# Holding the filter loads back until half of x has landed, with more filler matmuls in the first inverse stage

## The chip, the cores and the metric

The kernel runs on one core of a Trainium2 chip. The metric is device time in microseconds (us) of one execution. Beside the time, each execution has a span (first to last instruction, about 1.8 us less than the time) and the mean granted TensorE clock, 1.000 being full speed.

## The reference

x is [8, 3008, 256]. Along its sequence axis it goes through a real FFT, a product with a complex filter, and the inverse FFT. The result, 24064 tokens of 256, goes through a gated feed-forward layer.

```python
X = np.fft.rfft(x, axis=1)
Y = X * (filt_r + 1j * filt_i)[None]
y = np.fft.irfft(Y, n=3008, axis=1).reshape(24064, 256)
out = (np.maximum(y @ w_gate, 0) * (y @ w_val)) @ w_out      # d_ff = 1536
```

## The kernel before

The FFT is done in matmul stages. For the first of the eight batches they run one after the other, before the feed-forward stage has anything to do: **A** (psA: x times a DFT table, evicted to asb, stored to DRAM as Abuf), the reload of Abuf as **at** in another layout, **B** (psX: a small DFT of at; tt and uu: products with the filters Ftr and Fti; psD: the inverse, with the tables I2t and I2u; evicted to dsb, stored as Dbuf), and C (psY). I2t is a rearranged F2 and I2u is I2t times a permutation, both built on chip while the loads run. Fillers ("junk", psJ) are matmuls whose results nobody reads; they are there to keep TensorE's clock up.

The order of the opening:

```python
q = NX2 * D // 4                                     # a quarter of one of the two x tiles
next(filters)                                        # first of eight filter loads, at once
load_x(0, nc.sync, ((0, 0, q), (0, q, 2 * q), (0, 2 * q, 4 * q), (1, 0, 2 * q), (1, 2 * q, 4 * q)))
# ...
load_own_filters()
hold_gpsimd(XF[0][:, 2 * q - 8:2 * q])               # GpSimd reads x, so its DMA issues wait
for _ in filters:                                    # the seven other filter loads (casts to bf16)
    pass

warm(11)
for i, f in enumerate(items_a(0)):                   # A: 16 matmul pairs on x
    f()                                              # ... loads of at in between
# ...
for half in range(2):
    for a in range(2):
        place_filter(0, a, half, nc.vector.tensor_copy)   # VectorE copies Ftr: needs its landing
for i in range(3):
    make_back_t(i)                                   # TensorE -> psI, VectorE -> I2t
warm(6)
place_filter(1, 0, 0, nc.vector.tensor_copy)
for i in range(3):
    make_back_u(i)                                   # TensorE reads I2t; ScalarE -> I2u
# ... three more copies of Fti
for i in range(15):
    warm(2)                                          # 30 fillers, a fixed count

def amid(i):                                         # between the groups of B
    if i < 2:
        warm(4, 256)
    else:
        ...                                          # psA of the second batch

hold_gpsimd(ats[0][0:32, NG - 1, 0:8])               # GpSimd waits for at
load_vg(0, DFF // 2)
first_b(amid)
```

`hold_gpsimd` is a tiny GpSimd copy that reads the named columns; GpSimd's later DMA issues stand behind it in order.

## Time and profile before

| | before |
|---|---|
| time, median of 3 executions | 896.22 us (895.55 to 896.71) |
| span of the profiled execution, clock | 895.1 us, 0.998 |
| GpSimd's hold on x passes | 9.52 us |
| VectorE begins to copy the whole real filter | 23.11 us |
| last x part seen by TensorE | 22.48 us |
| at has landed (GpSimd's hold on it passes) | 36.11 us |
| first psX (B begins) | 36.08 us |
| first psY (C begins) | 59.63 us |

The next fence is the DMA view of the kernel before, first for 13 to 16 us, then for 19 to 23 us. q0 is GpSimd's queue (the filters), q1 SyncE's (x, Abuf, at); the columns are packets, MB, and share of the time of 16 engines.

```profile
q0 software_dynamic: 401, 0.35, 76.6%
q1 hardware_dynamic: 68, 0.37, 36.9%
...
q1 hardware_dynamic: 307, 0.75, 57.4%
q0 software_dynamic: 322, 0.24, 41.2%
```

### The profile page before, as it was taken

To read this page: it belongs to the slowest core of one execution; us is meant where nothing else is said; L and a number is where in the kernel's file an instruction comes from. 1 tells how busy PE (TensorE), PEld (TensorE's weight loads), DVE (VectorE), ACT (ScalarE), POOL (GpSimd) and SP (SyncE) were. 2 spreads that over 40 slices of the span, in tenths; PEclk is the share of its full clock that TensorE was granted. 3 is DMA by queue.
4 is the path that set the end of the run, shared out by engine and by line. 5 is a ranking of instruction groups with operands and counts; after the bars stand their busy time and mean duration, and the time that the engine had idled before them with its cause. 6 is when DMAs were issued, how large, how long until landed. Compare 5 with 4: busy or idle time off the path is not lost.

```text
span 895.1 us, 19152 instructions
## 1 busy us (share of the span) xinstructions
PE 878.4 (98%) x7206; PEld 507.2 (57%) x7206; DVE 569.2 (64%) x873; ACT 498.8 (56%) x891; POOL 364.4 (41%) x361
## 2 busy tenths in 40 slices
PE   7999999999999999999999999999999999999997
PEld 2335555556556665566655566555655566566665
DVE  2637766577665776666766676657776577655553
ACT  3475555555555556556555556555655555555552
POOL 4351698038661486416672167802867000000001
PEclk9999999999999999999999999999999999999999
DMA  8998448434466336463375334762445512331111
GB/s 229 281 242 170 131 132 179 110 102 121 122 152 135 117 95 146 129 139 94 97 175 139 92 99 108 179 139 78 118 138 148 121 31 80 81 74 36 37 34 51
DMA packets 114099, 109.18 MB, mean 122 GB/s; under 512 B 20359, under 2 KB 98599, under 8 KB 113366
## 3 DMA queue, kind: packets, MB, share of 16 engines
q1 hardware_dynamic: 90294, 80.10, 34.7%
q0 software_dynamic: 22992, 26.41, 12.3%
q8 instruction: 57, 0.93, 0.5%
q10 hardware_dynamic: 720, 1.45, 0.5%
q14 instruction: 36, 0.29, 0.1%
HBM read 61.93 MB, written 49.81 MB: 125 GB/s over the span
## 4 chain that ended last, share of the span: by engine, by line
PE 94%; DMA 2%; ACT 1%; POOL 1%; SPq 1%; DVE 1%; issue 1%; ACTq 0%; POOLq 0%
PE psV L467 28%; PE psG L467 27%; PE psO L486 27%; PE psF L323 3%; PE psD L394 2%; PE psY L451 2%; PE psX L364 2%; PE psA L276 1%; DMA XF<-in_x_dram 1%; PE psJ L520 1%; SPq L176 1%; DVE prod L472 0%; ACT dsb L401 0%; DMA dC<-Dbuf 0%; POOL out_dram L509 0%
## 5 line engine op out<-in xcount | busy, mean ns | idle before, releaser
L472 DVE SCALAR_TENSOR_TENSOR prod<-psG,vsb 128x512 bf16<-128x512 f32 x564 | 389.0, 690 | 263.4 <-ACT vsb L470 257.5
L470 ACT CAST vsb<-psV 128x512 bf16<-128x512 f32 x564 | 331.9, 589 | 263.2 <-PE psV L467 162.8
L467 PE MATMUL psV<-yT,WvT 128*128 128x512 bf16 x1128 | 336.6, 380 | 0.8 <-ACT asb L330 0.5
L486 PE MATMUL psO<-WoT,prod 128*128 128x256 bf16 x2256 | 336.5, 273 | 0.0
L467 PE MATMUL psG<-yT,WgT 128*128 128x512 bf16 x1128 | 335.5, 379 | 0.9 <-ACT dsb L401 0.3
L486 PEld LDWEIGHTS <-prod 128*128 128x128 bf16 x2256 | 220.3, 98 | 143.7
L467 PEld LDWEIGHTS <-WgT 128*128 128x128 bf16 x1128 | 109.9, 97 | 136.4 <-issue 3.4
L467 PEld LDWEIGHTS <-WvT 128*128 128x128 bf16 x1128 | 98.5, 98 | 41.8 <-issue 30.5
L258 POOL CAST scr<-prod 128x8 f32<-128x8 bf16 x24 | 4.5, 189 | 257.7 <-DVE prod L472 257.7
L509 POOL DMA_DIRECT2D out_dram<-osb x5 | 2.6, 536 | 195.9 <-ACT osb L499 195.9
L499 ACT COPY osb<-psO 128x512 f32<-128x512 f32 x92 | 53.9, 586 | 28.0 <-PE psO L486 26.6
L380 DVE TENSOR_TENSOR tt<-psX,Ftr 128x512 bf16<-128x512 f32 x96 | 65.1, 682 | 6.8 <-PE psX L364 6.8
L309 POOL TENSOR_TENSOR fold<-XP 128x1024 f32<-128x1024 f32 x24 | 56.6, 2357 | 20.8 <-PE psF L323 19.4
L380 DVE TENSOR_TENSOR uu<-psX,Fti 128x512 bf16<-128x512 f32 x89 | 60.5, 680 | 0.0
L401 ACT CAST dsb<-psD 128x512 bf16<-128x512 f32 x96 | 51.5, 589 | 12.5 <-PE psD L394 12.4
L296 POOL DMA_DIRECT2D XP<-in_x_dram x96 | 56.7, 596 | 3.2 <-PE psG L467 1.6
L310 POOL TENSOR_TENSOR XP<-XP 128x1024 f32<-128x1024 f32 x24 | 56.4, 2349 | 1.9
L330 ACT CAST asb<-psF 128x512 bf16<-128x512 f32 x48 | 25.8, 589 | 30.5 <-PE psF L323 30.5
L330 DVE CAST asb<-psF 128x512 bf16<-128x512 f32 x48 | 30.9, 686 | 18.6 <-PE psF L323 18.6
L456 ACT CAST yT<-psY 128x512 bf16<-128x512 f32 x47 | 27.5, 586 | 22.9 <-PE psY L451 22.6
L458 DVE CAST yT<-psY 128x512 bf16<-128x512 f32 x47 | 32.0, 681 | 9.7 <-PE psY L451 9.7
L451 PE MATMUL psY<-M,dC 96*128 96x94 bf16 (+18 forms) x604 | 37.5, 199 | 0.5 <-DMA dC<-Dbuf 0.4
(70 smaller groups left out, 493.3 us busy)
## 6 DMA issues: line engine op xcount, KB each, us to landing
at<-Abuf SPq DMA_DIRECT2D x32, 384.0 KB
dC<-Dbuf SPq DMA_DIRECT2D x64, 192.0 KB
XP<-in_x_dram POOLq DMA_DIRECT2D x48, 256.0 KB, 5.9
Dbuf<-dsb SPq DMA_DIRECT2D x23, 512.0 KB
XP<-in_x_dram POOLq DMA_DIRECT2D x96, 96.0 KB, 2.6
Abuf<-asb SPq DMA_DIRECT2D x96, 96.0 KB
out_dram<-osb SPq DMA_DIRECT2D x69, 94.0 KB
XF<-in_x_dram SPq DMA_DIRECT2D x15, 256.0 KB
```

The lines of the kernel that those rows point to most:

```text
L296: nc.gpsimd.dma_start(xp[r:r + 24, 0:4:2, :], _ap(x, (b * N1 * N2 + o) * D, [[N2 * D, 24], [47 * N2 * D, 2], [1, 512]]))
L309: tt(t, xp[:, 0:2], xp[:, 2:4], op=ALU.add)
L310: tt(xp[:, 2:4], xp[:, 0:2], xp[:, 2:4], op=ALU.subtract)
L330: copy(asf[:, :, q, :], banks[q])
L380: nc.vector.tensor_tensor(p, psX, filt, op=ALU.mult)
L401: nc.scalar.copy(dsb[:, a, o:o + 2, :], psD[a])
L451: nc.tensor.matmul(psY[:, o:o + w], dCs[b, n2 // 8][:, n2 % 8, h * 128:(h + 1) * 128], M1[:, n1:n1 + w], start=True, stop=True)
L467: nc.tensor.matmul(pt[:, :W], w[:, h, ft * 128:(ft + 1) * 128], yt[:, h, :], start=(h == 0), stop=(h == 1))
L470: nc.scalar.copy(vsb, psV[:, :W])
L472: nc.vector.scalar_tensor_tensor(prod, in0=psG[:, :W], scalar=0.0, in1=vsb, op0=ALU.max, op1=ALU.mult)
L486: nc.tensor.matmul(psO[:, t % 2], prods[ft][:, t * 128:(t + 1) * 128], WoT[:, ft, :], start=(ft == 0), stop=(ft == NFT - 1))
L499: copy(osb[:, t0 % 2:t % 2 + 1], psO[:, t0 % 2:t % 2 + 1])
```

## The change

The intent is to let x, which is on the path through A, Abuf and at, have the DMA engines for longer before the filters join, and to cover a stretch of B in which TensorE idles and its clock falls.

```diff
-    hold_gpsimd(XF[0][:, 2 * q - 8:2 * q])
+    hold_gpsimd(XF[0][:, 4 * q - 8:4 * q])
@@ def amid(i):
         if i < 2:
-            warm(4, 256)
+            warm(6, 256)
```

On TensorE this adds four 128x256 filler matmuls; no engine's other instructions change their order.

## The prediction

> **What bounds the kernel now.** I first read the page's busy shares, then the busy times in two long stretches, to see where a change in the opening could count at all.
>
> ```profile
> PE 878.4 (98%) x7206; PEld 507.2 (57%) x7206; DVE 569.2 (64%) x873; ACT 498.8 (56%) x891; POOL 364.4 (41%) x361
> 0.00:36.00 36.00, 28.69 (x130) 10.65 (x130) 15.24 (x25) 12.14 (x20) 10.45 (x20) 1.00 0.90 245
> 62.00:895.00 833.00, 825.57 (x6881) 486.57 (x6878) 542.76 (x830) 467.67 (x836) 339.68 (x324) 1.00 0.45 113
> ```
>
> The columns of the last two lines are the stretch, its length, busy PE, weight loads, DVE, ACT, POOL, the granted clock, the DMA share and GB/s. After 62 us TensorE is busy 825.6 of 833 us and nothing in the diff reaches there. So the change acts only in the opening, and a shift of the opening goes through to the end about one to one. Next, the chain of waits up to the first B:
>
> ```profile
> 13.49 8.74 DMA XF<-in_x_dram
> 22.48 3.65 PE psA L276 x8
> 28.94 6.49 PE psJ L520 x30
> 35.43 0.65 issue
> 36.08 0.46 PE psX L364 x8
> ```
>
> The reader is to see two things: x's last part lands at 22.24 us, and the first B (psX) begins at 36.08, straight after 30 filler matmuls that have a fixed count. Why did those begin only at 28.8? The timelines of TensorE and of VectorE answer (start, length, operation, count, idle before it and what ended that):
>
> ```profile
> 26.73 1.47 PE L520 MATMUL psJ<-junk 128*128 128x512 bf16 x6
> 28.04 0.91 PE L202 MATMUL psI<-I2t,tabs 128*128 128x512 bf16 x3
> 28.78 6.64 PE L520 MATMUL psJ<-junk 128*128 128x512 bf16 x30
> 36.08 0.41 PE L364 MATMUL psX<-at,F 64*64 64x256 bf16 x8 [0.66 <-PE psJ L520]
> ```
>
> ```profile
> 17.85 0.95 DVE L238 COPY Ftr<-Ftr 32x3072 bf16<-32x3072 bf16 x1 [11.52 <-DMA Ftr<-in_filt_r_dram]
> 23.11 2.90 DVE L238 COPY Ftr<-Ftr 32x3072 bf16<-32x3072 bf16 x3 [4.30 <-DMA Ftr<-in_filt_r_dram]
> 26.43 2.08 DVE L197 CAST I2t<-psI 128x256 bf16<-128x256 f32 x6 [0.42 <-PE psI L192]
> ```
>
> VectorE waits for the real filter until 23.11, copies it to 26.01, and only then makes I2t. TensorE's three I2u matmuls read I2t, and the 30 fillers stand behind them. The x path (psA done at 26.13) and the filter path (copies done at 26.01) meet within 0.2 us: the kernel is balanced there. Where the fillers end, the load of "at" has also just landed: GpSimd's own hold on it starts at 36.11. So three things end together, and the slack of the fillers is about 0.65 us.
>
> Last, the granted clock in stretches of 3.41 us around the first B:
>
> ```profile
> 34.28:37.69 3.41, 2.75 (x30) 1.23 (x27) 1.17 (x2) 0.00 (x0) 1.28 (x3) 1.00 0.95 297
> 37.69:41.10 3.41, 2.02 (x28) 0.95 (x26) 3.11 (x6) 2.02 (x4) 2.33 (x3) 1.00 0.92 281
> 41.10:44.52 3.42, 3.42 (x27) 1.36 (x26) 1.43 (x3) 2.83 (x7) 3.42 (x4) 0.50 1.08 359
> ```
>
> After a stretch with gaps the clock is halved for exactly one stretch. This is what the extra filler is aimed at.
>
> **What the Trainium skill says.** "TensorE: Matmul & The Clock Gate", Part 1 (What's actually happening): the clock falls to half after an idle window of 3413 ns, the windows run freely, and one busy window restores it. The trace agrees: clock 0.50 from 41.10 to 44.52 us. The opening fillers also run 0.43 us apart (11 in 4.72 us) up to 7.0 us, and later ones 0.22 us apart (30 in 6.64 us), though the clock column reads 1.00 in both places. The same page (Architectural detail) says that ScalarE and VectorE are strict FIFO; VectorE's timeline above has I2t behind the filter copies. "DMA: Bandwidth & Descriptors", Queues, rings and completion order: each DMA engine takes turns between queues packet by packet. The trace agrees: from 13 to 23 us x and the filters both advance, at about 170 and 87 KB per us. The same page (SWDGE vs HWDGE vs iDMA) ties casts to DMAs of GpSimd; the filters are cast to bf16 and are indeed issued from there, so they cannot pass to another queue.
>
> **The change part by part.**
>
> First, the hold. GpSimd's hold copy starts at 9.52 us in the trace, TensorE's matmuls on the second half of the first tile (the data that the new hold names) start at 13.07 us. The seven remaining filter DMAs, issued from 10.01 to 13.8 us, are therefore issued about 13.6 to 17.4 us: 3.6 us later. In the trace their first packets in number appear at 13.0 us, three us after the first issue, so they should now appear near 16.6 us.
>
> What x gains: from 13.0 to 16.6 us it has the DMA engines alone. From 9.49 to 13.07, when it was nearly alone, the engines moved 291 GB/s; from 13 to 23 us its queue had 0.17 MB per us. Of the 1.54 MB that remain at 13 us it moves about 0.98 MB by 16.6 and the other 0.56 MB at the mixed rate in 3.3 us: x is complete at about 20, some 2.3 us earlier, and psA ends near 23.7 instead of 26.13.
>
> What the filters lose: the last DMA of the real filter, issued at 11.09, took 11.9 us to land (23.0). From the first packet to that landing some 1060 packets passed in 10 us, about 105 per us beside x, and 138 per us at 26 us beside the loads of "at", whose packets are small. Moved by 3.6 us and slightly sped up by x being gone sooner (my estimate: 0.6 us), it lands at 26.0, not 23.0. Then, with the measured durations: three copies to 29.0 (2.90); I2t to 31.1 (2.08); the last I2u matmul and first filler near 31.3 (in the trace the fillers begin 0.27 after I2t ends); 30 fillers, 6.5, to 37.8; first B at 37.85. That is 1.8 us later than 36.08. What x gained is lost in a wait of TensorE: psA, I2t's matmuls and six fillers are done by about 25.8, and it then has nothing until I2t's first third is there, at 29.7.
>
> That gap of about 3.9 us, followed by three short matmuls to 31.3, is long enough to halve the clock. At half clock seven of the 30 fillers run 0.43 us apart in one window and cost about 1.5 us more: first B at 39.3, 3.2 us later. I give this a chance of 0.55. The mean of the two is +2.6 us.
>
> "at" itself should land about when it did (36): from 13 to 31.5 us the DMA share is near or over 1, so what x takes earlier the filters take later, out of the Abuf stores and "at" loads.
>
> Second, the filler. Two groups get two more 128x256 matmuls each, 4 x 0.107 = 0.43 us of TensorE. They lie ahead of the third psX and before the wait for GpSimd's first product (uu, done at 40.27); TensorE idles 0.35 and 0.93 us there, so the filler costs nothing on the path. It raises the activity of the window that led to the throttle. I take the streaming time alone in 37.69 to 41.10 (fillers 0.05, psX 0.24, inverse 0.43, psA 0.34) as 1.06 of 3.41 us, 31%; 10.38 to 13.80, with about 1.6 us, 47%, did not throttle. With the filler and a later start of B the window has about 1.5, 44%, between the two: a chance of a half. Without the throttle, B saves about 1.2 us, not the whole 1.7 us of half clock, because GpSimd's products (five in 5.63 us from 39.11) bound the second and third inverse. Half of 1.2 is 0.6 us.
>
> Sum of the main line: 896.2 + 2.6 - 0.6 = 898.2 us.
>
> **The rivals.** (1) The change works as meant: x earlier makes Abuf and "at" earlier, and the filters come in quickly once x is through, because their queue can be fast (378 packets in one us at 71 us, nearly alone). For it speaks that the last x landing is on the chain of waits; against it, that Abuf and "at" follow x in the queues at once and leave no quiet stretch, and that the fillers' count is fixed. With the clock kept it would give about 895.2 us (-1.0). I give it one in five. (2) The hold changes nothing visible, since three paths meet at 36 us and the filters catch up within the 0.65 us of slack; only the clock decides: 895.0 to 896.2. This needs the filter landing before about 23.7, hardly possible with an issue 3.6 us later. (3) The wait on I2t takes the place of the wait on x, the clock falls in it, and B is throttled again by the shifted windows: 36.08 + 3.2 and no saving, 899.4 to 900.5.
>
> **Range and chances.** Weighing the main line 0.8 and rival 1 with 0.2: 0.8 x 898.2 + 0.2 x 895.2 = 897.6 us. The range from 894.4 to 900.6 covers rival 1 with a saved clock at one end and rival 3 at the other. A change of 2% would be 18 us, more than half the opening; no step here is near it, so within 2% is nearly sure.
>
> **What would show each step.** Hold: GpSimd's filter issues at 13.6 us. x: the last psA group starting near 20.2. Filters: VectorE's long copy group starting near 26, I2t near 29. Fillers: a gap of three to four us on TensorE ahead of the I2u matmuls, ended by VectorE, and the 30 fillers lasting 6.6 us (clock kept) or 8 us (clock halved). First psX at 37.8 to 39.3. B: clock 1.00 where it was 0.50. I am wrong if the first psX starts before 36 us, which would mean that the filters' late issue was made up by a faster queue, or if the time from the first psX to the last one's inverse grows with the filler.

## The result, and the profile after

The changed kernel took 895.67 us in the median of 4 executions (894.82 to 896.64), the kernel before 895.88 (895.24 to 896.71, 4 executions). The ratio is 0.9998 with a 95% interval of 0.9980 to 1.0015. Ratios here and below are the mean time of one kernel's fast runs over that of the other's of the same rounds, so not quite the ratio of the medians quoted.

The time is inside my range, but I had forecast 1.4 us more and got 0.2 us less; the profile shows which steps of the sum were wrong. The chain of waits of the changed kernel, up to the first B:

```profile
8.20 3.77 DMA XF<-in_x_dram
...
12.13 0.19 POOL scr L258
...
14.76 9.27 DMA Fti<-in_filt_i_dram
24.03 0.96 DVE Ftr L238
...
28.71 7.53 PE psJ L520 x30
36.23 0.40 PE psX L364 x8
```

The chain used to run through x's last landing. Now it runs through the hold, a filter load, VectorE's filter copies, I2t and the fillers: the wait on the filters has taken the place of the wait on x. (The profile infers a load of Fti as the releaser of a copy of Ftr here. VectorE's timeline below names a load of Ftr and shows no wait after 23.06, so I read this step as "the filters" and not as that one load.) Yet the fillers begin at 28.5 us, not at 31.3 as I had worked out. The timelines of VectorE and TensorE of the changed kernel:

```profile
20.36 0.95 DVE L238 COPY Ftr<-Ftr 32x3072 bf16<-32x3072 bf16 x1 [14.02 <-DMA Ftr<-in_filt_r_dram]
23.06 2.90 DVE L238 COPY Ftr<-Ftr 32x3072 bf16<-32x3072 bf16 x3 [1.75 <-DMA Ftr<-in_filt_r_dram]
25.99 2.08 DVE L197 CAST I2t<-psI 128x256 bf16<-128x256 f32 x6
```

```profile
12.10 10.51 PE L276 MATMUL psA<-XF,WA 128*96 128x512 f32 x24 [1.06 <-DMA XF<-in_x_dram]
26.80 0.39 PE L202 MATMUL psI<-I2t,tabs 128*128 128x512 bf16 x1 [2.12 <-DVE I2t L197]
28.50 7.74 PE L520 MATMUL psJ<-junk 128*128 128x512 bf16 x30
36.16 0.41 PE L364 MATMUL psX<-at,F 64*64 64x256 bf16 x8
```

The whole real filter is there at 23.06, as before (23.11), although its load was issued 2.6 us later in this profile. psA runs through from 12.10 to 22.6 us without a wait, 3.5 us ahead of before. at has landed at 35.16:

```profile
35.16 0.18 POOL L258 CAST scr<-at 32x8 f32<-32x8 bf16 x1 [18.73 <-DMA at<-Abuf]
```

That is one microsecond earlier than before, but the first psX still starts at 36.16, because the 30 fillers took 7.74 us and not 6.64. The granted clock shows why (stretches of one window; columns as in the prediction):

```profile
23.89:27.30 3.41, 1.19 (x5) 0.30 (x4) 3.33 (x7) 0.07 (x1) 0.00 (x0) 1.00 1.12 244
27.30:30.71 3.41, 3.18 (x8) 1.04 (x8) 3.23 (x8) 1.69 (x3) 0.00 (x0) 0.50 1.13 348
```

The wait on I2t leaves a window with 1.19 us of work, and the window after it is at half clock, right in the fillers. In B, where the kernel before lost its window (41.10 to 44.52), the clock now stays at 1.00; the piece from the first psX to the end of the last eviction of B takes 16.67 us instead of 17.25. So one halved window has moved from B into the fillers.

Why did the filters catch up? The DMA view of the changed kernel for the same two stretches, 13 to 16 us and 19 to 23 us:

```profile
q1 hardware_dynamic: 161, 0.88, 90.8%
q0 software_dynamic: 1, 0.00, 2.3%
...
q0 software_dynamic: 545, 0.54, 80.6%
q1 hardware_dynamic: 163, 0.54, 36.6%
```

x moves 0.88 MB in the first stretch instead of 0.37, as predicted. In the second the filters move 0.54 MB instead of 0.24. SyncE's queue then has less to ask for. By the packets in the traces, x's last one ends at 17.6 us in the changed kernel and at 21.9 us in the kernel before, while the filters' come in number from 16.2 us: the two run side by side for little more than one microsecond. The Abuf stores that follow become ready only as psA makes them, one store of 393 KB per four psA matmul pairs, that is per 3.4 us (eight matmuls in 3.64 us in the kernel before). That is 0.115 MB per us, where x took 0.17. My prediction had let the filters go on at their old rate.

### The profile page after: what moved, and what is told of

It reads as the page before. It is cut to its first block, busy times and chain, and to the rows that moved or that the text cites. A ratio compares the mean times of both kernels' runs of the same rounds, so it can differ in the third digit from the quotient of the medians.

```text
span 894.9 us, 19039 instructions
## 1 busy us (share of the span) xinstructions
PE 871.8 (97%) x7090; PEld 508.0 (57%) x7210; DVE 569.0 (64%) x873; ACT 499.4 (56%) x891; POOL 364.6 (41%) x361
## 4 chain that ended last, share of the span: by engine, by line
PE 85%; DVE 4%; ACT 4%; DMA 3%; issue 1%; POOL 1%; SPq 1%; POOLq 0%; ACTq 0%; DVEq 0%
PE psG L467 26%; PE psO L486 25%; PE psV L467 24%; DVE prod L472 3%; PE psF L323 3%; ACT vsb L470 3%; PE psD L394 2%; PE psX L364 2%; PE psY L451 2%; DMA at<-Abuf 1%; DMA Fti<-in_filt_i_dram 1%; PE psJ L520 1%; SPq L340 1%; ACT dsb L401 0%; DMA XF<-in_x_dram 0%
## 5 line engine op out<-in xcount | busy, mean ns | idle before, releaser
L467 PE MATMUL psG<-yT,WgT 128*128 128x512 bf16 x1107 | 330.7, 379 | 6.9 <-DVE prod L472 0.8
L467 PE MATMUL psV<-yT,WvT 128*128 128x512 bf16 x1030 | 315.2, 380 | 0.8 <-ACT asb L330 0.5
L309 POOL TENSOR_TENSOR fold<-XP 128x1024 f32<-128x1024 f32 x24 | 56.5, 2356 | 20.5 <-PE psF L323 19.4
L456 ACT CAST yT<-psY 128x512 bf16<-128x512 f32 x47 | 27.6, 586 | 22.9 <-PE psY L451 22.7
```

What stands on the lines that cost most here:

```text
L309: tt(t, xp[:, 0:2], xp[:, 2:4], op=ALU.add)
L467: nc.tensor.matmul(pt[:, :W], w[:, h, ft * 128:(ft + 1) * 128], yt[:, h, :], start=(h == 0), stop=(h == 1))
```

## The experiments

All twelve runs were correct. Kernels are compared only within the same rounds. A clock of 0.999 or 1.000 went, in every profile I have, with no halved window in the opening; 0.997 and less went with one or more; 0.998 had one in the two profiles that show it (the last window, after the last matmul, lowers the mean a little too and costs nothing).

| run | median us | ratio to before (95%) | first psX | filter there | at there |
|---|---|---|---|---|---|
| before_again | 896.06 | 0.9996 (0.9983 to 1.0009) | 35.85 | 21.30 | 35.71 |
| after_again | 895.11 | 0.9984 (0.9972 to 0.9996) | 35.14 | 22.69 | 35.17 |
| hold_only | 897.10 | 1.0005 (0.9991 to 1.0019) | 36.33 | 22.80 | 35.75 |
| filler_only | 895.76 | 0.9991 (0.9979 to 1.0003) | 36.81 | 22.49 | 36.84 |
| hold_3q | 897.57 | 1.0015 (1.0003 to 1.0027) | 39.40 | 25.27 | 37.18 |
| hold_full | 899.08 | 1.0034 (1.0021 to 1.0047) | see text | 26.38 | see text |
| fill_gap | 895.85 | 1.0000 (0.9988 to 1.0012) | 35.78 | 21.73 | 35.81 |
| t_first | 895.31 | 0.9998 (0.9986 to 1.0011) | 35.25 | other order | 35.28 |
| filler_12 | 895.88 | 1.0007 (0.9992 to 1.0023) | 34.96 | 22.77 | 34.99 |
| at2_early | 894.57 | 0.9989 (0.9975 to 1.0003) | 35.07 | 22.85 | 35.10 |
| both_waits | 893.64 | 0.9980 (0.9966 to 0.9994) | 35.07 | other order | 35.10 |
| after_third | 895.63 | 1.0002 (0.9988 to 1.0016) | 35.63 | 23.11 | 35.66 |

"Filter there" is the start of VectorE's second group of copies of the real filter; in t_first and both_waits these copies stand behind I2t and say nothing of the landing.

### Both kernels again

No edit: the kernel before and the changed one, to see how steady their profiles are.

> The kernel before, unchanged, to see in how many of its runs the clock is halved for a window and what a halved window costs. My theory (both kernels lose one clock window of 3.41 us in those executions whose free-running window falls on a gap, and only then): runs fall in two groups, granted clock 1.000 with a span near 893.8 us and 0.998 with a span near 895.1; the halved window, where there is one, lies in the first B (41 to 45 us). Rival (each run of the kernel before is throttled in B, so the change has removed a steady loss): all runs 0.998, span near 895.1 throughout.

> The changed kernel, unchanged. My theory: two groups again, clock 1.000 with spans of 893.0 to 893.3 us and 0.998 or less with 894.3 to 894.9; the real filter lands near 23 us again in the profile, TensorE waits about 2 us for I2t ahead of the I2u matmuls, and the at load lands near 35.2. Rival (the early landing of the filters was chance): the filter lands near 26 us as I predicted, and the first psX starts at 38 us or later.

In the kernel before, the halved window is not always in B. In this profile it lies at 17.59 to 21.01 us, behind the wait for x:

```profile
18.12 8.51 PE L276 MATMUL psA<-XF,WA 128*96 128x512 f32 x16 [2.56 <-DMA XF<-in_x_dram]
```

So the theory was right that the windows fall where they happen to fall, and wrong that B was their place. Of 38 executions of the kernel before, 13 had a clock of 0.997 or less, 18 of 0.998 and 7 of 0.999 or more. Of the changed kernel's 15 (three sets), it was 5, 1 and 9. Two groups of times, as expected, did not appear: the means of those three classes of the kernel before are 896.34, 895.94 and 895.69 us, less apart than the executions within a class. In this second profile of the changed kernel no window was halved in the opening, and the earlier at goes through:

```profile
27.97 6.64 PE L520 MATMUL psJ<-junk 128*128 128x512 bf16 x30
35.14 0.41 PE L364 MATMUL psX<-at,F 64*64 64x256 bf16 x8 [0.53 <-PE psJ L520]
```

The fillers take 6.64 us and end before at is there. The filter's early landing was no chance: 22.69 here.

### The two parts alone

```diff
# hold_only: the changed kernel with
-            warm(6, 256)
+            warm(4, 256)
# filler_only: the kernel before with
-            warm(4, 256)
+            warm(6, 256)
```

> The later hold alone, filler of before (4). My theory: filters issued near 12.6 us still land near 23; a wait of about 2 us on I2t; at lands near 35.2, one us earlier than before; first psX near 35.2 to 36.2, depending on whether the clock is halved in that wait. B is more often throttled than with the filler of 6. Time 893.0 to 895.0 in the runs without a halved window, mean within 0.2% of before. Rival (late filters cost): psX at 38, time 898.

> The longer filler alone, hold of before. My theory: TensorE's 0.43 us more of filler is hidden in the wait for the first product of GpSimd, so first psX near 36.1 and the first inverse's second half near 40.3 as before; no halved window in B, hence a gain of about 0.5 us in the runs where before would have been throttled, and none in the others: 895.2 to 895.9 mean. Rival (the filler lies on the path): the second half of the first inverse starts 0.4 us later and the time rises by 0.4 us.

The hold alone has the I2t wait (1.52 us) and the earlier at, and in its profile a halved window at 28.39 to 31.81 us, in which the fillers stretch to 8.32 us; psX at 36.33 is therefore later than at (35.75). Four of its six executions had a clock of 0.993 to 0.997, and their times reach 899.64 us; the mean, 897.19, is above what I had expected. The later hold by itself gains nothing and is exposed to the clock.

The filler alone costs nothing that can be seen: its B takes 16.66 us with a full clock, as the kernel before takes in B with a full clock (16.67, before_again). Its profiled execution did lose a window, but behind the wait for x (18.07 to 21.48 us), as in before_again. The other four of its five executions had 0.999 or more, against one of 16 of the kernel before. Its psX started late, at 36.81, because at landed late in that execution (36.84); that is the spread of the landing, not the filler.

Hold_only's mean is 1.9 us above the changed kernel's (895.33, five executions), more than one halved window costs. With six executions that spread over 5 us I do not explain that difference.

### How far the hold can be moved

```diff
-    hold_gpsimd(XF[0][:, 4 * q - 8:4 * q])
+    hold_gpsimd(XF[1][:, 2 * q - 8:2 * q])      # hold_3q
+    hold_gpsimd(XF[1][:, 4 * q - 8:4 * q])      # hold_full
```

> Changed kernel, filters held until three quarters of x have landed. My theory (the filters caught up because psA hands Abuf stores to the SP queue at only one 393 KB store per 3.4 us once x is through, so the DMA engines are free for them; the order changes, the last landing hardly does): issue moves some 2 to 3 us to about 15.5 us, but the real filter lands only 1 to 2 us later, near 24 to 25; TensorE waits 3 to 4 us for I2t; first psX at 36 to 38; 895 to 897 us. Rival of my prediction (the filters move one to one with their issue): landing 25.5 or later, psX from 38.5, 897 us or more.

> Filters held until all of x has landed. Theory: with no x left beside them the filters run at well over the 105 packets per us of the kernel before; issue near 18.5 us, first packets near 21.5, real filter landed 6 to 7 us after that issue plus 3, near 27 to 28 us; I2t ready then plus 5, fillers behind it, psX near 39 to 41; clock nearly always halved in the wait; 898 to 901 us. Here the delay is real, since no slack is left. Rival (work is conserved whatever the order): real filter still before 25, psX before 38, 896 us.

The hold passes at 15.26 us (three quarters) and 17.64 us (all). In the three profiles with the quarter it passed at 8.86 us on average and the filter was there at 22.30; in the nine with the half it passed at 12.44, and in the seven of them that show the landing the filter was there at 22.72. So 3.6 us of later issue cost 0.4 us of landing; the next 2.8 us cost 2.6 us. The time from hold to landing is 13.4 us with the quarter (12.9 to 13.8), 10.3 with the half (9.1 to 10.9), and in one profile each 10.0 with three quarters and 8.7 with all, the last in the odd execution told of below. Only the first step is clear of the spread. That step is the one that takes x out of the filters' way: x's last packet ends at 19.8 to 21.9 us with the quarter and at 17.2 to 17.6 with the half. In hold_3q it ends at 16.6 us, before the filters' first packet (17.0), so a later hold finds nothing more to take away.

My expectation of 24 to 25 us for hold_3q was thus wrong, and the rival's (25.5 or later, psX from 38.5) close. From three quarters on, the slack is gone and the loss that I had predicted for the change appears. TensorE waits 4.20 us for I2t, two windows are halved, and the fillers end 2.2 us after at has landed (37.18):

```profile
29.01 1.90 PE L202 MATMUL psI<-I2t,tabs 128*128 128x512 bf16 x3 [4.20 <-DVE I2t L197]
30.71 8.76 PE L520 MATMUL psJ<-junk 128*128 128x512 bf16 x30
39.40 0.41 PE L364 MATMUL psX<-at,F 64*64 64x256 bf16 x8
```

The profiled execution of hold_full fell in a state I had not met: its mean granted clock was 0.557 (0.56 from about 8.3 us on) and its span 1517.3 us. It is left out of every comparison of time; the median and the ratio in the table are over the five fast ones (897.52 to 899.82). Its filter landing is from that odd execution, in which psA and so the Abuf stores were slower too; it may be early for that reason. Its psX and at are not read. The five fast times lie at the low end of the expected 898 to 901 us; the expected landing and psX can't be judged.

### Taking away the gap before I2u

```diff
# fill_gap: the changed kernel, ahead of the I2u matmuls
-    warm(6)
+    warm(16)
# t_first: the changed kernel, I2t ahead of the filter copies
+    for i in range(3):
+        make_back_t(i)
     for half in range(2):
         for a in range(2):
             place_filter(0, a, half, nc.vector.tensor_copy)
-    for i in range(3):
-        make_back_t(i)
...
-    for i in range(15):
+    for i in range(21):
         warm(2)
```

> Changed kernel with 16 in place of 6 fillers ahead of the I2u matmuls, where TensorE now waits 1.4 to 2.1 us for I2t; 10 more are 2.16 us. Theory (what is left of the change's gain depends on the clock being halved in that gap): no run has a halved window at 27 to 31 us; first psX at 35.2 in the profile; spans 892.7 to 893.5 in all runs, granted clock 0.998 or more; 0.2 to 0.3% below before. Rival (the two groups of spans have another cause, such as DMA landing times alone): spans spread as with the changed kernel, 892.7 to 895.1, or all 0.4 us longer because I2u now starts later.

> I2t made ahead of the four copies of the real filter on VectorE, so that it no longer waits for the filter's landing; 42 in place of 30 fillers behind it to bridge the wait for at. Theory: I2t starts near 23.2 us, no wait of TensorE, I2u matmuls by 25.5, fillers to about 34.7, first psX at the landing of at, 35.2; no halved window; spans 892.7 to 893.5, as fill_gap and not better, since at sets the start of B. Rival (the filter path still sets it): psX later than 36, because the copies of the filters, now behind I2t, end later than at lands.

The clock part came true: all eleven executions had 0.999 or 1.000, and neither profile shows a halved window in the opening. The I2t wait is gone in t_first, where VectorE's I2t starts at 23.09 us instead of 25.99, and psX starts at the landing of at, as it does in fill_gap. But the spans still spread from 892.9 to 895.8 us, and neither is measurably faster than the kernel before (1.0000 and 0.9998). The rival is half right: the clock is not the only thing that scatters the time. Subtracting the first psY from later landmarks shows a second place. In the profiles of the changed kernel, fill_gap and t_first (psX 36.16, 35.78, 35.25) TensorE loses 0.7 to 1.0 us near 184 us; in before, before_again, after_again, hold_only and filler_only it does not. This is the wait list of TensorE between 100 and 890 us for the changed kernel:

```profile
PE psX L364 <- DMA at<-Abuf: 0.8, 1, 0.8
PE psG L467 <- ACT dsb L401: 0.5, 1, 0.5
PE psV L467 <- ACT asb L330: 0.5, 1, 0.5
```

The third batch's at, loaded in the middle of the feed-forward stage, lands just about when it is needed, sometimes late. The diff does not touch this load. But the four profiles that lose time there (after_third is the fourth) all have the half hold, and none of the three with the quarter does; with so few, whether the hold makes the late landing likelier stays open.

### The filler doubled

```diff
-            warm(6, 256)
+            warm(12, 256)
```

> Changed kernel with the filler in B doubled, 6 to 12 matmuls in each of the two groups: 12 x 0.107 = 1.28 us more of TensorE work. Theory (the filler lies in the wait for GpSimd's first product, which starts 4.23 us after the first psX whatever TensorE does): from the first psX to the start of the last Dbuf store 16.7 us, as with 4 and 6 (16.70 and 16.69 in the runs with the full clock), at most 0.2 us more. Rival (filler is on the path): 17.9 us, and the time 1.2 us longer.

B, from the first psX to the end of its last eviction, takes 16.90 us, against 16.67 with six fillers (the expectation's 16.70 was read at the store that follows). Of 1.28 us of added TensorE work 0.23 us is seen, and even that is not the filler: the last pair of evictions but one starts 13.96 us after the first psX, as in the changed kernel (13.97), and the last pair then waits 0.25 us for an earlier store of Dbuf. The filler is hidden, with room for about twice as much.

### The third batch's load earlier, and both waits removed

```diff
# at2_early: the changed kernel with
-            for j, e in enumerate((-74, -69, -62, -55) if b == 2 else (-74, -69, -64, -57)):
+            for j, e in enumerate((-74, -69, -62, -57) if b == 2 else (-74, -69, -64, -57)):
# both_waits: the same edit on t_first
```

> Changed kernel with the last part of the third batch's first stage, and with it the load of at behind it, two steps (2.6 us) earlier. Theory (a part of the spread that hid the gain is a wait of TensorE for that load near 184 us, 0.6 to 1.0 us in three of the nine profiles that I compared, none in the others): no wait there; the piece from the first psY to the end of TensorE 829.7 us, as in the good profiles. Mean 0.3 to 0.5 us below the changed kernel. Rival (the wait comes from elsewhere and is moved): 830.5 us or more again, or a new wait for the fold at 158 us.

> I2t ahead of the filter copies with 42 fillers, and the third batch's load two steps earlier: a version meant to beat both. Theory: no halved window in the opening, psX at the landing of at (35.2 to 35.8), psY to the end of TensorE 829.7; spans 892.5 to 893.5 in all runs; 0.2% below before in the same call. Rival (the landing of the first at and of the last output set the spread): spans 892.7 to 895 again, no gain over the changed kernel.

> The changed kernel once more beside these, on the same chip. Theory: mean of spans 893.6, in two groups by the halved window (0.999 or more: 892.7 to 893.6 where at of the third batch is in time; 0.998 and less: 893.3 to 895.1); mean 0.05 to 0.15% below before. Rival (no difference from before at all): ratio 1.000.

The edit moves the last part of the third batch's A, and the loads behind it, two steps earlier. In at2_early the piece from the first psY to the end of TensorE is 829.10 us. I had expected 829.7: beside the wait for at, a constant wait of 0.5 us of psV on an asb eviction near 162 us, which every profile had that I compared, is gone as well. Its mean is 894.55 us, against 895.67 for the changed kernel (after_third).

Both_waits, with I2t first as well, is the fastest: 893.64 us, ratio 0.9980 to before with an interval that excludes 1, spans from 891.2 to 893.0, and 0.999 or more in all six executions. It beats both kernels, by 0.2%. Its profiled execution, the slowest of the six, still has one late landing (0.8 us on a dC load near 143 us), and its piece from the first psY to the end is 830.06 us, not the 829.7 expected. After_third gave 1.0002: not distinguishable from before. Its profile loses about 1.1 us near 184 us again (830.84 us from the first psY to the end, against 829.7 to 829.8 in the profiles without that wait), and 0.5 us in B at full clock (17.19 us), where ScalarE waits for an earlier store to free its buffer:

```profile
51.74 1.07 ACT L401 CAST dsb<-psD 128x512 bf16<-128x512 f32 x2 [0.54 <-DMA Dbuf<-dsb]
```

## Why the prediction was right or wrong

**The bound and the size of the effect: right.** Nothing after 62 us depended on the diff, and no step was near 2%.

**The hold and x: right in the issue, low in the gain.** On the average of the profiles the hold moved by 3.58 us (12.44 less 8.86), the 3.6 of the prediction. x was to be complete at about 20 us; its last packet ended at 17.6. One cause is a wrong reading: 1.54 MB, the second x tile, were taken as remaining at 13 us, but SyncE's queue had moved 1.99 MB by then, nearly all of it x, which is 3.08 MB in all, so 1.1 to 1.2 MB remained. psA was to end at 23.7 us and ended at 22.6, since x was never late again after 12.10.

**The filters' landing: wrong, and this is the step that failed.** The prediction had "Moved by 3.6 us and slightly sped up by x being gone sooner (my estimate: 0.6 us), it lands at 26.0, not 23.0". It landed at 22.7 on average; the speeding up was 3.2 us, not 0.6. The rate of 105 packets per us was a rate beside x, and x was through little more than a microsecond after the filters began. From 19 to 23 us the filters had 136 packets per us (545 in 4). That the time from hold to landing falls from 13.4 to 10.3 us when x is taken out of the way, and no further in hold_3q, is measured; that it is the pace of the Abuf stores, released by psA, which kept the room free afterwards is argued from the byte counts and not tested by itself.

**The loss of 1.8 us in the fillers: wrong with it.** TensorE's wait on I2t exists, but was 1.4 to 2.1 us and not 3.9, and the fillers end before or about when at lands, if the clock holds. hold_3q shows the predicted loss where the filter really is 2.6 us late.

**at landing when it did: wrong.** It came 0.9 us earlier: 35.34 us in the mean of the nine profiles with the half hold, 36.22 in the three with the quarter. I had argued that what x takes early the filters take later out of the Abuf stores and at loads. The byte counts suggest that they took it from slack in SyncE's queue, which rival 1 would have needed and which I denied it ("leave no quiet stretch").

**The halved clock in the wait: right, with its size.** It occurred in one of three profiles of the changed kernel and in hold_only, and cost 1.1 us (7.74 less 6.64) and 1.7 us (8.32 less 6.64); I had said about 1.5. fill_gap and t_first, which fill or remove the wait, show no sign of it in eleven executions.

**The filler: right in being hidden, high in its gain.** Saving the window in B is worth 0.58 us (17.25 less 16.67) and not 1.2. I had also taken the halved window in B for a property of the kernel before; in its other profile it lay at 17.6 us. Whether the filler saves the window is only in part shown. B ran at full clock with four fillers too, in before_again and hold_only; the clocks of filler_only (four of five at 0.999 or more, against one of 16 of the kernel before) speak for it.

**The rivals and the sign of being wrong.** Rival 2 came nearest: its range (895.0 to 896.2) and its condition, the filter there before about 23.7 us, were both met, though I had called the condition hardly possible. Rival 1 was right that at lands earlier, and rival 3 that the wait on I2t takes the place of the wait on x. The sign that I had named, the first psX before 36 us, shows in after_again (35.14) and after_third (35.63), and not in the first profile (36.16), where the halved window hid it.

**The sum.** I had +2.6 and -0.6, shaded to 897.6. The terms that the runs show are 0.9 us gained at the first B, of which a halved window takes back 1.1 to 1.7 us in those executions where one falls on the I2t wait, and 0.6 us gained in those where the kernel before would have lost its window in B. Over all executions the changed kernel's mean is 895.56 us (15) and the kernel before's 896.03 (38); these are pooled, so the 0.5 us is only indicative, and each interval but one includes no change. The range held by luck: the errors were small beside it, and the main line was wrong.

## What to carry to other kernels

When one transfer is put behind another, do not move its landing by the delay of its issue: ask who shares the engines with it in its new place, and how fast the work that follows can ask for more. A gain of one microsecond at a balanced point can vanish in the wait that takes its place; here that was the table built behind the filter copies. Closing that wait alone did not show in the time either (t_first, 0.9998); only together with the earlier load of the third batch did it (both_waits, 0.9980). Where the effect is as small as the spread, subtract landmarks between several profiles before explaining anything: a part of the scatter here sat near 184 us, far from any line of the diff.

## What the Trainium skill lacked or had wrong

- "TensorE: Matmul & The Clock Gate", Part 1 and HAM oscillation: it names an idle window, and as a rule "no PE-idle gaps >~3.4µs". Here windows with work in them were followed by a halved one: 1.19 of 3.41 us busy by the profile (a gap of 2.12 us) in the changed kernel, 1.34 in hold_only, 1.39 in before_again, 2.02 in B of before, where small matmuls and gaps of 0.35 and 0.93 us alternate. Windows with 1.77 and 1.96 us (10.38 to 13.80 and 20.62 to 24.04 us, before) were not, so the busy share of the profile alone does not tell them apart. The page has a second case, short idle times between groups of matmuls, but gives no share of activity at which the clock falls. Its window length agrees: 3.42 us in the first profile. The prediction's "The trace agrees" holds for that length and the half clock, not for an idle window.
- The same page says that the windows run freely and that the count of slow matmuls at a kernel's start differs from run to run for this reason. It does not say that a kernel can lose a window in different places later on: the kernel before lost one at 41.1 us in one execution and at 17.6 us in another, and a halved window cost 0.6 to 1.7 us depending on where it fell.
- The same page mentions a clock stuck at a quarter for 50 us and more. In one execution here (hold_full) the granted clock stood at 0.56 from about 8.3 us to the end of the 1517.3 us; the page names no state of that size.
- "DMA: Bandwidth & Descriptors", Latency and other measured facts: about 1 us to the first byte of a load issued from GpSimd. Here the first filter packet after the hold came 1.3 us after the issue in hold_3q (15.75 and 17.0 us) and hold_full (18.13 and 19.4), where x had ended by then, but 2.6 us after it in the kernel before (10.01 and 12.6) and over 3 us in the changed kernel (12.62 and about 16), where x was still moving. The page gives no figure for this time beside other work.
